# Local attention and two mixing layers on one core: a byte limit on loads in flight, and the constant matmuls that fill gaps

## The chip, the core and the metric

The kernel runs on one core of a Trainium2 chip. The core's engines run side by side and wait for each other only through semaphores: TensorE (PE, with its weight loads shown apart as PEld), VectorE (DVE), ScalarE (ACT), GpSimd (POOL) and SyncE (SP), which here issues every DMA. The metric is the device time of one execution in microseconds (us), as the median of several runs.

## What is computed

The reference chains three layers over 2 sequences of 768 positions and 512 channels (8 heads of 64). Cut to what matters:

```python
k_sum = k.reshape(B, H, nb, 32, D).max(axis=3)       # 24 blocks of 32 keys
v_sum = v.reshape(B, H, nb, 32, D).mean(axis=3)
scores = concat(window of |i-j| < 16, q @ k_sum.T + log(32))
x = softmax(scores) @ concat(v, v_sum)               # heads side by side: 512 channels
theta = x @ w_theta
y = w_tok_r @ (x * cos(theta)) + w_tok_i @ (x * sin(theta))
u = x + y;  x = u + relu(u @ w_ch)
h = gelu(x @ w_in);  u, v = halves(h);  v = normalised(v) * g
out = x + (u * (w_sg @ v + b_sg)) @ w_out
```

The large products are made of three matmuls each (high by high, high by low, low by high parts), lines 352 to 354 of the kernel.

## The kernel before, in words

The work is cut into named steps. Each step has an engine, and one long text, PLAN, lists all steps in the order in which they are issued; `play` goes through it and calls each step's function. Every engine works off its own steps strictly in that order, and an instruction that waits holds up all behind it on its engine. SP's queue is such an engine too: a load that waits holds up all later loads.

Attention handles eight pairs of heads (0 to 7; 0 to 3 are the first sequence), each in two halves of the sequence. For pair p and half h the steps are: loads `kp`, `vTp`, `qp_h`, `vp_h` (384 KB, 384 KB, 192 KB, and two of 97 and 194 KB); `ksp` on DVE, the maxima over blocks of 32 keys (line 514); `Sp_h` on PE, the scores (`scores`: 4 matmuls that write the mask, line 558, then 24 on q and k, line 565, then 24 on q and `ksp`, line 572, as the trace counts them); `m` and `d` on DVE (lines 578 and 599), `e` on ACT (line 607), `PT` on PE (transposes, line 613), `Pt` (their copies out), `O` on PE (line 627), `n` on DVE and `X` on PE (line 649). `vs`, `vp`, `vm`, `vr` carry the block means of v from POOL through PE and ACT into the tiles that `O` reads. From about 41 us the steps `th` (x by w_theta) run between those of attention, and from 70 us those of the token mix (`y`). The loads of weights are `wth`, `wr`, `wi` and `wri`; each is followed by `t` on ACT (line 459) and `r` on DVE (line 466), which put the number together from its two 16-bit parts.

Three things in this stage are touched by the change:

- Loads. Each is a plain `nc.sync.dma_start` (lines 453, 480, 498, 500, 503 and 509). There are eight DMA semaphores, used in turn, so a load waits until the eighth load ahead of it has landed; that is the only limit on loads in flight, apart from buffers that have to come free.
- `fill` (function `filler`, line 405): 8 matmuls of 512 columns on a tile of zeros, right at PE's start. Nothing reads their result. Every `S` step stands behind it on PE.
- `idle0` to `idle4` (function `keep_busy`, line 411): matmuls of 480 columns on constant tiles, whose result nothing reads either. `IDLE` says how many each has: 8, 1, 2, 5, 1. `idle0` stands behind the fifth score step `S1_0`, `idle1` and `idle2` among the first transposes, `idle3` ahead of `S3_0`, `idle4` ahead of `O3_1`.

Of the kernel before, what the change touches and what calls it, by code (L numbers as in the profile page):

```python
# [58 lines left out]
d3_0_0.V.294 m3_0_1.V.2 Pt2_1_0.A.528 vT1.S.696 d3_0_1.V q3_1.S.672 S3_1.P.2.7 e1_0.A PT1_0_0.P.1
vs1.G.6 PT1_0_1.P.3 m3_1_0.V.3 d3_1_0.V.339 vT2.S.624 vp1.P.6 vs2.G.5 vp2.P.4 m3_1_1.V.2 d3_1_1.V  # L60
wth0t.A.0 Pt0_0_1.A.72 e2_0.A PT2_0_0.P.0 vm1.A.1 wth1d.S.896 v0_0.S.847 v0_1.S.798 v1_1.S.1103
v1_0.S.1054 wth3d.S.990 vr0_0.G Pt1_0_0.A.774 vr0_1.G PT2_1_1.P.6 O0_0_0.P.1 v2_0.S.1295 vr1_0.G
O0_0_1.P vp3.P.5 wth1t.A.1 O0_1_0.P.2 O0_1_1.P Pt2_0_0.A.504 n0_0.V.4.198 vr1_1.G O1_1_0.P.0
vm2.A.0 e3_0.A PT3_0_0.P.7 PT3_0_1.P.4 Pt1_0_1.A.0 PT2_0_1.P.1 v2_1.S.1246 vr2_1.G vm3.A.1
# [6 lines left out]
th0_1.P n2_1.V.2 v3_1.S.1655 vr3_1.G idle4.P.5 O3_1_0.P.5 n3_0.V.4 O3_1_1.P X2_1.P.7 xe2_0.A
X3_0.P.1 wth3r.V.1504 th1_1.P th2_1.P xe0_1.A wri2d.S.1591 wi0t.A.1 wth2l.V xh0_1.A.720 q7_0.S.1567
k5.S.1872 n3_1.V.4 xh2_0.A.144 xe1_1.A wr0t.A.0 X3_1.P.5 wri1d.S.1808 k4.S.1760 ks4.V.2 xe3_0.A
wth3h.G.64 S4_0.P.1.0 xl2_0.G xl0_1.G th0_2.P xe2_1.A S4_1.P.7.2 vT4.S.2064 xe3_1.A ks5.V.4
wri0d.S.2000 xh3_0.A.672 wr0r.V.1472 m4_0_0.V.3 wth3l.V d4_0_0.V.1427 wri0t.A.2 xl3_0.G m4_1_0.V.2
m4_0_1.V.3 th1_2.P th2_2.P vs4.V.5 th1_3.P th0_3.P th4_0.P.1 d4_0_1.V vp4.P.0 xh3_1.G.528
# [1008 lines left out]
```

## Time and profile before

| | |
|---|---|
| three runs, median | 386.76 us (386.74 to 387.22) |
| the profiled execution's own time | 386.78 us |
| its span, first to last instruction | 384.9 us |
| PE busy (matmuls) | 371.5 us, 97% |
| DVE, POOL, ACT busy | 281.9, 219.9, 171.4 us |
| DMA | 40.5 MB, mean 105 GB/s |

The span is 1.9 us shorter than the execution's time, which also has a start and an end around it. The page cuts the span into 40 slices of 9.6 us. In the first six slices the DMA engines are nearly always busy (77% to 100%, 258 to 376 GB/s), and from the eighth on they are mostly idle. PE's clock shows below full in the first, second and third slice and is full from there. The last stage of the page, the chain of work that ended last, has PE in 88% of it.

### The profile page before, as it was taken

How to read it: one execution, taken by the hardware profiler on the slowest of the kernel's cores; microseconds unless marked ns; L12 is line 12 of the kernel's file. 1: busy time of each engine (PE TensorE's matmuls, PEld its weight loads, DVE VectorE, ACT ScalarE, POOL GpSimd, SP SyncE). 2: the span in 40 equal slices, each digit the busy share in tenths (PEclk: the TensorE clock that was granted, in tenths of full speed). 3: DMA queues.
4: the chain of work that ended last, by engine and by line, in shares of the span. 5: the costliest groups of instructions: out<-in, count | busy, mean ns of one | idle time of the engine just before them, and what ended most of it. 6: DMA issues, size and time to landing. Idle time of an engine off the chain costs nothing.

```text
span 384.9 us, 7757 instructions
## 1 busy us (share of the span) xinstructions
PE 371.5 (97%) x3073; PEld 333.3 (87%) x3073; DVE 281.9 (73%) x468; ACT 171.4 (45%) x321; POOL 219.9 (57%) x227
## 2 busy tenths in 40 slices
PE   6798999999999999999999999999999999999995
PEld 3577877988888888888889998899899999999994
DVE  4848899898797416954279999979655665368984
ACT  1258778987888635211033436545235102223510
POOL 5656585967454588639545336356632377683440
PEclk9689999999999999999999999999999999999999
DMA  7989997050632230000175350000001000000116
GB/s 269 376 258 346 353 336 232 22 179 6 214 111 72 93 128 35 2 2 2 54 261 190 109 177 3 0 2 1 2 0 41 2 0 2 0 2 0 41 43 246
DMA packets 16483, 40.50 MB, mean 105 GB/s; under 512 B 2240, under 2 KB 7872, under 8 KB 16448
## 3 DMA queue, kind: packets, MB, share of 16 engines
q1 hardware_dynamic: 16448, 40.01, 30.7%
q8 instruction: 24, 0.39, 0.4%
q14 instruction: 11, 0.09, 0.1%
HBM read 36.86 MB, written 3.15 MB: 104 GB/s over the span
## 4 chain that ended last, share of the span: by engine, by line
PE 88%; DVE 6%; issue 2%; ACT 2%; DMA 1%; SPq 0%; DVEq 0%; ACTq 0%
PE bank L352 25%; PE bank L353 25%; PE bank L354 24%; PE bank L627 3%; PE bank L613 3%; PE bank L565 2%; PE bank L649 1%; PE bank L414 1%; PE bank L572 1%; DMA page0F<-in_kT_dram 1%; DVE xT L899 1%; DVE page8R L347 1%; PE bank L558 1%; DVE page7R L347 1%; DVE page12F L813 0%
## 5 line engine op out<-in xcount | busy, mean ns | idle before, releaser
L578 DVE TENSOR_REDUCE small<-bank 128x3 f32<-128x360 f32 x32 | 16.4, 524 | 5.8 <-PE bank L572 5.7
L742 DVE TENSOR_TENSOR xT<-bank,xT 128x512 f32<-128x512 f32 (+1 forms) x16 | 8.3, 547 | 6.5 <-PE bank L354 6.5
L956 ACT ACTIVATE page6F<-bank 128x384 f32<-128x384 f32 x8 | 3.9, 489 | 18.8 <-PE bank L354 18.8
L347 POOL TENSOR_TENSOR page3R<-xT,page3R 128x384 fp32r<-128x384 f32 x6 | 6.8, 1128 | 8.3 <-ACT page3R L339 5.7
L347 POOL TENSOR_TENSOR page2R<-xT,page2R 128x384 fp32r<-128x384 f32 x7 | 7.1, 1025 | 6.5 <-ACT page2R L339 4.2
L973 DVE SCALAR_TENSOR_TENSOR page1F<-bank,g_sb,page10F 128x384 f32<-128x384 f32 x8 | 4.7, 613 | 8.3 <-PE bank L354 8.3
L339 ACT ACTIVATE page10R<-page4F 128x512 fp32r<-128x512 f32 (+1 forms) x2 | 1.5, 740 | 20.0 <-PE bank L353 19.9
L979 POOL TENSOR_TENSOR page1F<-page1F,page6F 128x384 f32<-128x384 f32 x6 | 6.6, 1113 | 5.9 <-DVE page1F L973 4.7
L347 POOL TENSOR_TENSOR page2R<-page9F,page2R 128x512 fp32r<-128x512 f32 x6 | 8.7, 1446 | 1.7 <-ACT page2R L339 1.5
L341 POOL TENSOR_SCALAR page2R<-page9F 128x512 fp32r<-128x512 f32 (+1 forms) x4 | 2.7, 672 | 11.8 <-PE bank L354 9.8
L347 POOL TENSOR_TENSOR page1R<-page9F,page1R 128x512 fp32r<-128x512 f32 x2 | 4.6, 2312 | 7.2 <-ACT page1R L339 7.2
L352 PE MATMUL bank<-page0R,page2R 128*128 128x512 f32 (+1 forms) x21 | 8.5, 405 | 0.0
L347 POOL TENSOR_TENSOR page8R<-page10F,page8R 128x512 fp32r<-128x512 f32 (+1 forms) x3 | 4.6, 1522 | 6.3 <-ACT page8R L339 6.3
L354 PE MATMUL bank<-page0R,page2R 128*128 128x512 f32 (+1 forms) x21 | 7.8, 373 | 0.0
L607 ACT ACTIVATE page1F<-page1F 128x720 f32<-128x720 f32 x4 | 3.2, 800 | 10.4 <-DVE page1F L599 10.4
L353 PE MATMUL bank<-page0R,page2R 128*128 128x512 f32 (+1 forms) x21 | 7.8, 371 | 0.0
L558 PE MATMUL bank<-maskb,identb 64*64 64x288 bf16 x64 | 5.2, 315 | 2.0 <-DVE identb L390 2.0
L466 DVE SCALAR_TENSOR_TENSOR page9F<-page9F,stage 128x512 int32<-128x512 int32 x2 | 1.4, 690 | 7.7 <-POOL page1R L347 7.7
L339 ACT ACTIVATE xT<-bank 128x384 f32<-128x384 f32 x11 | 5.2, 490 | 3.8 <-PE bank L649 3.8
L347 POOL TENSOR_TENSOR page3R<-page4F,page3R 128x512 fp32r<-128x512 f32 x2 | 2.6, 1308 | 7.1 <-ACT page3R L339 7.1
L459 ACT ACTIVATE stage<-page11F 128x512 f16<-128x512 bf16 x8 | 6.2, 786 | 0.9 <-DVE page7F L466 0.9
L1000 POOL TENSOR_TENSOR page10F<-page10F,xT 128x384 f32<-128x384 f32 x3 | 3.6, 1184 | 5.2 <-ACT page10F L339 5.2
(1066 smaller groups left out, 1627.9 us busy)
## 6 DMA issues: line engine op xcount, KB each, us to landing
page11F<-in_w_rT_dram SPq DMA_DIRECT2D x3, 511.8 KB, 5.3
page11F<-in_w_iT_dram SPq DMA_DIRECT2D x3, 511.8 KB, 5.4
page13F<-in_w_in_dram SPq DMA_DIRECT2D x3, 511.8 KB, 5.2
out_dram<-page10F SPq DMA_DIRECT2D x7, 192.0 KB, 2.0
page6F<-in_w_in_dram SPq DMA_DIRECT2D x2, 511.8 KB, 3.4
out_dram<-page1F SPq DMA_DIRECT2D x5, 192.0 KB, 2.1
page6F<-in_vW_dram SPq DMA_DIRECT2D x4, 193.5 KB, 4.3
page0F<-in_kT_dram SPq DMA_DIRECT2D x2, 384.0 KB, 5.0
```

What stands on the lines that cost most here:

```text
L339: ACT.activation(dst, src, AF.Copy)
L347: EN[e].tensor_tensor(out=lo, in0=src, in1=hi.bitcast(F32), op=ALU.subtract)
L352: PE.matmul(ps, ah, bh, start=first, stop=False, skip_group_check=True)
L353: PE.matmul(ps, ah, bl, start=False, stop=False, skip_group_check=True)
L354: PE.matmul(ps, al, bh, start=False, stop=last, skip_group_check=True)
L558: PE.matmul(s3(h)[sl(ab, 64), :, :WK], identb[rr, rr], maskb[rr, m:m + 3], start=True, stop=False, skip_group_check=True)
L565: PE.matmul(s3(h)[sl(ab, 64), t, :WK], q[rr, sl(2 * t + ab, 64)], k[rr, FIRST[w]:FIRST[w] + WK], start=False, stop=True, skip_group_check= ...
L578: op(f"m{u}_{h}", "V", lambda e, h=h: DVE.tensor_reduce(out=T(f"m{u}_{h}"), in_=s3(h), axis=AX.X, op=ALU.max, negate=True), after=[f"S{u}" ...
L613: PE.transpose(T(f"PT{u}_{h}")[:WC, sl(t)], T(f"P{u}")[:, 360 * h + t * WC:360 * h + (t + 1) * WC], ident)
L627: PE.matmul(ps[64 * ab:64 * ab + 64, o:o + 65], sb[:WC, t * P + 64 * ab:t * P + 64 * ab + 64], v[:WC, c:c + 65], start=True, stop=True)
L742: DVE.tensor_tensor(out=dst, in0=ps, in1=dst, op=ALU.add)
L979: op(f"gm{b}_{th}_{f}", "VG", lambda e, gf=gf, s=s, ut=ut: EN[e].tensor_tensor(out=T(gf)[:, s], in0=T(gf)[:, s], in1=T(ut), op=ALU.mult), ...
```

## The change

A new constant, `FLIGHT`, and a function `fetch` that all the loads on lines 453, 480, 498, 500, 503 and 509 now go through (those of g, of `w_sg` and `b_sg`, and the stores, do not). `fetch` issues the load and then counts back over the loads before it, newest first: as soon as those counted make 850,000 bytes, the next older one is made a condition, and this load waits until that one has landed. So when a load is issued, the loads ahead of it that may still be on their way are as many as it takes to reach 850,000 bytes. The wait for the eighth load back stays.

`fill` becomes 80 matmuls of 48 columns, each with its own load of 128 columns of weights, on the same tile of zeros. `IDLE` goes from (8, 1, 2, 5, 1) to (4, 1, 3): `idle0` has 4, the one that stood between `PT0_0_0` and `PT0_1_0` is gone, the next has 1 in place of 2, the one ahead of `S3_0` has 3 in place of 5, and the one ahead of `O3_1` is gone. The order of all other steps is as it was.

```diff
-IDLE = (8, 1, 2, 5, 1,)
+FLIGHT = 850_000
+
+IDLE = (4, 1, 3,)
...
-m2_1_1.V.0 m1_0_1.V.3 d2_1_1.V idle0.P.3 PT0_0_0.P.4 m1_0_0.V.1 idle1.P.3 PT0_1_0.P.1 e1_1.A
-idle2.P.3 PT1_1_0.P.5 Pt0_1_0.A.0 vT3.S.222 d1_0_0.V.2715 d1_0_1.V vT0.S.528 k3.S.480 ks3.V.1
+m2_1_1.V.0 m1_0_1.V.3 d2_1_1.V idle0.P.3 PT0_0_0.P.4 m1_0_0.V.1 PT0_1_0.P.1 e1_1.A idle1.P.3
+PT1_1_0.P.5 Pt0_1_0.A.0 vT3.S.222 d1_0_0.V.2715 d1_0_1.V vT0.S.528 k3.S.480 ks3.V.1 PT0_0_1.P.0
...
+    flying = []
+
+    def fetch(dst, src):
+        i = nc.sync.dma_start(dst, src)
+        i = getattr(i, "ins", i)
+        left = FLIGHT
+        for n, name in reversed(flying):
+            if left <= 0:
+                tc.add_manual_dep(i, name, mybir.DependencyInfo(
+                    mybir.DependencyClass.Sync, mybir.DependencyReason.DATA), reason="flight")
+                break
+            left -= n
+        flying.append(((2 if dst.dtype == I16 else 4) * math.prod(dst.shape), i.name))
...
     def filler(e):
         ps, warm = T("warmb"), T("warm", BF16)
-        for j in range(8):
-            PE.matmul(ps, warm[:, :P], warm[:, P:640], start=True, stop=True)
+        for j in range(80):
+            PE.matmul(ps[:, :48], warm[:, :P], warm[:, P:P + 48], start=True, stop=True)
...
-                nc.sync.dma_start(raw[:, c:c + n - 1], w[:, 1:])
+                fetch(raw[:, c:c + n - 1], w[:, 1:])
...
-        op(f"k{p}", "S", lambda e: nc.sync.dma_start(T(f"k{p}"), kT[b, r]),
+        op(f"k{p}", "S", lambda e: fetch(T(f"k{p}"), kT[b, r]),
```

On SP's queue the loads stand in the same order; what they wait for differs. Before, from the fourth DMA on (in `[waits ...]` the semaphore of the load that must have landed; in_kT is a `k`, in_qT a `q`, in_vT a `vT`, in_w_theta a `wth`):

```order
L498 DMA page0F<-in_kT_dram 128x768
L503 DMA page0F<-in_qT_dram 128x384 x3
L503 DMA page1F<-in_qT_dram 128x384
L500 DMA page1F<-in_vT_dram 128x768 [waits DMAHW0_49]
L500 DMA page2F<-in_vT_dram 128x768 [waits DMAHW1_49]
L498 DMA page2F<-in_kT_dram 128x768 [waits DMAHW2_49]
L503 DMA page1F<-in_qT_dram 128x384 [waits DMAHW3_49]
L453 DMA page2F<-in_w_theta_dram 128x2047 [waits DMAHW4_49]
```

And now (all loads carry the line of `fetch`):

```order
L353 DMA page0F<-in_kT_dram 128x768
L353 DMA page0F<-in_qT_dram 128x384 [waits DMAHW0_49]
L353 DMA page0F<-in_qT_dram 128x384
L353 DMA page0F<-in_qT_dram 128x384 [waits DMAHW1_49]
L353 DMA page1F<-in_qT_dram 128x384 [waits DMAHW2_49]
L353 DMA page1F<-in_vT_dram 128x768
L353 DMA page2F<-in_vT_dram 128x768 [waits DMAHW4_49]
L353 DMA page2F<-in_kT_dram 128x768 [waits DMAHW6_49]
L353 DMA page1F<-in_qT_dram 128x384 [waits DMAHW7_49,DMAHW3_49]
L353 DMA page2F<-in_w_theta_dram 128x2047 [waits DMAHW0_49]
```

The fifth load waits for the first now, where it waited for none, and the load of weights (in_w_theta) waits for the ninth, four loads ahead of it, where it waited for the fifth.

On PE, among the first transposes (L613 before and L631 now are `PT` steps, L414 and L432 the `idle` ones). Before, behind the last matmul of `idle0`:

```order
L414 MATMUL bank3_66<-maskb_91,identb_90 128x480
L613 MATMUL bank4_67<-ident_89,page1F_191 120x128 x3
L414 LDWEIGHTS identb_90
L414 MATMUL bank3_66<-maskb_91,identb_90 128x480
L613 MATMUL bank1_64<-ident_89,page1F_191 120x128 x3
```

And now:

```order
L432 MATMUL bank3_66<-maskb_91,identb_90 128x480
L631 MATMUL bank4_67<-ident_89,page1F_263 120x128 x3
L631 MATMUL bank1_64<-ident_89,page1F_263 120x128 x3
L432 LDWEIGHTS identb_90
L432 MATMUL bank3_66<-maskb_91,identb_90 128x480
```

The second transpose step stands right behind the first. On PE's list of instructions the 72 more matmuls of `fill` and their 72 weight loads come first, so everything behind them stands 144 places later, less two for each `idle` matmul that is gone ahead of it.

## Rows read from the trace of the kernel before

**Rows 1.** The page, parts 1 and 4: busy time, and the chain by engine.

```profile
PE 371.5 (97%) x3073; PEld 333.3 (87%) x3073; DVE 281.9 (73%) x468; ACT 171.4 (45%) x321; POOL 219.9 (57%) x227
PE 88%; DVE 6%; issue 2%; ACT 2%; DMA 1%; SPq 0%; DVEq 0%; ACTq 0%
```

**Rows 2.** By stretch: length, busy (x instructions) by engine, clock, DMA share, GB/s.

```profile
7.00:12.95 5.95, 5.93 (x214) 5.56 (x214) 4.63 (x9) 0.68 (x1) 2.37 (x4) 0.71 1.05 403
15.35:20.50 5.15, 5.15 (x56) 3.19 (x57) 4.25 (x9) 0.80 (x1) 3.41 (x9) 0.50 1.01 320
20.50:30.00 9.50, 9.50 (x200) 7.80 (x198) 4.57 (x10) 6.46 (x15) 4.33 (x8) 0.94 0.84 260
30.00:47.30 17.30, 16.09 (x253) 13.72 (x251) 15.19 (x37) 13.79 (x29) 11.29 (x13) 1.00 1.02 355
100.00:384.90 284.90, 279.39 (x1571) 258.05 (x1565) 200.65 (x305) 104.40 (x195) 152.86 (x130) 1.00 0.17 58
```

**Rows 3.** Timeline, PE to 37 us: start, length, instruction, [idle before, releaser].

```profile
1.71 0.13 PEld L408 LDWEIGHTS <-page14F 128*128 128x128 bf16 x2 [1.71 <-DVE page14F L367]
1.72 3.29 PE L408 MATMUL bank<-page14F 128*128 128x512 bf16 x8 [1.72 <-DVE page14F L367]
2.12 0.15 PEld L408 LDWEIGHTS <-page14F 128*128 128x128 bf16 x1 [0.28 <-issue]
...
6.97 0.32 PE L558 MATMUL bank<-maskb,identb 64*64 64x288 bf16 x4 [1.97 <-DVE identb L390]
...
15.33 1.07 PE L565 MATMUL bank<-page0F 64*64 64x96 f32 x19 [2.41 <-issue]
...
36.66 0.92 PE L627 MATMUL bank<-page6F,page2F 120*64 120x65 f32 x23 [1.21 <-issue]
```

**Rows 4.** The chain that ended last, to 48 us: start, length, what; load `k1`, `idle` matmuls.

```profile
1.24 4.45 DMA page0F<-in_kT_dram
...
17.14 3.31 PE bank L414 x8
...
21.10 0.40 PE bank L414
...
21.95 0.41 PE bank L414 x2
...
25.31 1.01 PE bank L414 x5
...
43.80 0.22 PE bank L414
```

**Rows 5.** By stretch, PE and weight-load counts between the two stops; and DMA queues.

```profile
15.30:36.60 21.30, 20.11 (x376) 15.83 (x376) 15.07 (x36) 13.53 (x29) 13.11 (x23) 0.85 0.93 301
...
q8 instruction: 24, 0.39, 0.4%
```

**Rows 6.** DMA issues: count, KB each, us to landing; the third and fourth near their issue.

```profile
page14F<-in_kT_dram SPq DMA_DIRECT2D x1, 384.0 KB, 2.9
page4F<-in_w_theta_dram SPq DMA_DIRECT2D x1, 511.8 KB, 9.6
...
page9F<-in_kT_dram SPq DMA_DIRECT2D x1, 384.0 KB, 6.6
...
page12F<-in_w_rT_dram SPq DMA_DIRECT2D x1, 511.8 KB, 8.8
```

**Rows 7.** Timeline around `S4_0`: the issue of its load `k4`, `ks4` and `ks5`, `S4_0`.

```profile
36.26 0.43 SPq L498 DMA_DIRECT2D page9F<-in_kT_dram  x1
...
45.81 1.80 DVE L514 TENSOR_REDUCE small<-page9F 128x24 f32<-128x768 f32 x2
...
47.95 0.48 PE L572 MATMUL bank<-small,page8F 64*64 64x24 f32 x24
```

**Rows 8.** Timeline, DVE's waits for PE in the score stage.

```profile
16.62 0.53 DVE L599 TENSOR_TENSOR page0F<-bank,small 128x360 f32<-128x360 f32 x1 [0.87 <-PE bank L565]
...
24.18 0.97 DVE L578 TENSOR_REDUCE small<-bank 128x3 f32<-128x360 f32 x2 [3.40 <-PE bank L572]
...
27.49 0.53 DVE L578 TENSOR_REDUCE small<-bank 128x3 f32<-128x360 f32 x1 [1.46 <-PE bank L572]
```

**Rows 9.** Timeline: the load `wr1`, its steps on ACT and DVE, DVE's next waits.

```profile
47.26 0.74 SPq L453 DMA_DIRECT2D page12F<-in_w_rT_dram  x1
...
58.95 0.79 ACT L459 ACTIVATE stage<-page12F 128x512 f16<-128x512 bf16 x1
...
60.32 0.69 DVE L466 SCALAR_TENSOR_TENSOR page7F<-page12F,stage 128x512 int32<-128x512 int32 x1 [0.18 <-issue]
...
72.32 0.56 DVE L344 COPY xT<-bank 128x384 f32<-128x384 f32 x1 [0.81 <-PE bank L649]
```

More of the change, by code (lines that the diff above doesn't have):

```diff
@@ L59 @@
[L59 to L64, printed above, removed]
@@ L71 @@
[L71 to L76, printed above, removed]
@@ new lines @@
+PT1_1_0.P.5 Pt0_1_0.A.0 vT3.S.222 d1_0_0.V.2715 d1_0_1.V vT0.S.528 k3.S.480 ks3.V.1 PT0_0_1.P.0
+q2_0.S.198 S2_0.P.1.3 Pt0_0_0.A.123 m2_0_0.V.3 sets.G PT0_1_1.P.6 Pt1_1_0.A.456 PT1_1_1.P.5 vs3.G.4
+m2_0_1.V.2 d2_0_0.V.27 vs0.G.5 vp0.P.4 d2_0_1.V e2_1.A Pt0_1_1.A.96 Pt1_1_1.A.552 vm0.A.0
+wth0d.S.392 q3_0.S.744 PT2_1_0.P.2 idle2.P.6 S3_0.P.4.5 m3_0_0.V.3 d3_0_0.V.294 m3_0_1.V.2
+Pt2_1_0.A.528 vT1.S.696 d3_0_1.V q3_1.S.672 S3_1.P.2.7 e1_0.A PT1_0_0.P.1 vs1.G.6 PT1_0_1.P.3
+m3_1_0.V.3 d3_1_0.V.339 vT2.S.624 vp1.P.6 vs2.G.5 vp2.P.4 m3_1_1.V.2 d3_1_1.V wth0t.A.0
@@ new lines @@
+Pt0_0_1.A.72 e2_0.A PT2_0_0.P.0 vm1.A.1 wth1d.S.896 v0_0.S.847 v0_1.S.798 v1_1.S.1103 v1_0.S.1054
+wth3d.S.990 vr0_0.G Pt1_0_0.A.774 vr0_1.G PT2_1_1.P.6 O0_0_0.P.1 v2_0.S.1295 vr1_0.G O0_0_1.P
+vp3.P.5 wth1t.A.1 O0_1_0.P.2 O0_1_1.P Pt2_0_0.A.504 n0_0.V.4.198 vr1_1.G O1_1_0.P.0 vm2.A.0 e3_0.A
+PT3_0_0.P.7 PT3_0_1.P.4 Pt1_0_1.A.0 PT2_0_1.P.1 v2_1.S.1246 vr2_1.G vm3.A.1 v3_0.S.1197 X0_0.P.5
+wth0r.V.88 wth1r.V.1165 vr2_0.A Pt2_0_1.A.456 vr3_0.G O1_0_0.P.3 O1_0_1.P xe0_0.A e3_1.A O1_1_1.P
+n0_1.V.4.800 n1_0.V.2 n1_1.V.4 O2_1_0.P.5 O2_0_0.P.1 O2_0_1.P wth1h.G.2688 PT3_1_0.P.2 Pt2_1_1.A.0
@@ new lines @@
+O2_1_1.P Pt3_0_0.A.48 O3_0_0.P.7 n2_0.V.2 Pt3_0_1.A.24 O3_0_1.P wth2d.S.1472 wr0d.S.1408
+wth0h.G.576 X1_1.P.0 X1_0.P.4 X2_0.P.1 xh0_0.G.720 xl0_0.G wi0d.S.1344 wth2t.A.1 wth0l.V
+wth2r.V.1071 wth1l.V PT3_1_1.P.3 q4_1.S.966 wth3t.A.0 Pt3_1_0.A.1128 xe1_0.A xh1_0.A.672 xl1_0.G
+X0_1.P.2 Pt3_1_1.A.1104 th1_0.P.4 th0_0.P.6 wth2h.A.0 th2_0.P.3 q4_0.S.1704 th0_1.P n2_1.V.2
+v3_1.S.1655 vr3_1.G O3_1_0.P.5 n3_0.V.4 O3_1_1.P X2_1.P.7 xe2_0.A X3_0.P.1 wth3r.V.1504 th1_1.P
+th2_1.P xe0_1.A wri2d.S.1591 wi0t.A.1 wth2l.V xh0_1.A.720 q7_0.S.1567 k5.S.1872 n3_1.V.4
@@ new lines @@
+xh2_0.A.144 xe1_1.A wr0t.A.0 X3_1.P.5 wri1d.S.1808 k4.S.1760 ks4.V.2 xe3_0.A wth3h.G.64 S4_0.P.1.0
+xl2_0.G xl0_1.G th0_2.P xe2_1.A S4_1.P.7.2 vT4.S.2064 xe3_1.A ks5.V.4 wri0d.S.2000 xh3_0.A.672
+wr0r.V.1472 m4_0_0.V.3 wth3l.V d4_0_0.V.1427 wri0t.A.2 xl3_0.G m4_1_0.V.2 m4_0_1.V.3 th1_2.P
+th2_2.P vs4.V.5 th1_3.P th0_3.P th4_0.P.1 d4_0_1.V vp4.P.0 xh3_1.G.528 m4_1_1.V.6 d4_1_0.V.1763
+xh1_1.A.480 d4_1_1.V xl3_1.G wri1t.A.0 th2_3.P q6_1.S.1543 q6_0.S.1736 v4_0.S.1951 xl1_1.G
+q5_0.S.1927 S5_0.P.7.5 th4_1.P xh2_1.A.432 th5_0.P.2 xl2_1.G wr0h.A.960 wi0r.V.2080 e4_0.A
@@ new lines @@
+wri0r.V.1504 m5_0_1.V.6 m5_0_0.V.2 wr0l.G kk0.A.1696 d5_0_0.V.2019 th4_2.P PT4_0_0.P.7 vm4.A.1
+th4_3.P th5_1.P wri1r.V.1472 kk1.A.1664 wr2d.S.2240 e4_1.A d5_0_1.V PT4_0_1.P.5 th5_2.P wi1d.S.2176
+wi1t.A.2 PT4_1_0.P.0 vr4_0.G th5_3.P wr2t.A.1 wr3d.S.2112 kk2.A.1395 vT5.S.2448 Pt4_0_0.A.1371
+th3_0.P.7 rr1.V.352 vT6.S.2400 wr1d.S.2336 PT4_1_1.P.4 v4_1.S.2639 th3_1.P th3_2.P wr1t.A.0
+wi1r.V.1840 wr1r.V.1440 rr2.V.320 vr4_1.A rr0.V.1664 wri0h.G.1024 vs5.V.6 vp5.P.6 wr1h.G.1088
+Pt4_0_1.V.2312 v5_0.S.2590 wi2d.S.2526 k6.S.912 vs6.V.2 ks6.V.6 Pt4_1_0.A.1347 wi1h.G.128
@@ L479, in load @@
             for s in srcs:
-                nc.sync.dma_start(raw[:, c:c + s.shape[1]], s)
+                fetch(raw[:, c:c + s.shape[1]], s)
                 c += s.shape[1]
@@ L497, in at_pair @@
         b, r = divmod(p, NP)
-        op(f"k{p}", "S", lambda e: nc.sync.dma_start(T(f"k{p}"), kT[b, r]),
+        op(f"k{p}", "S", lambda e: fetch(T(f"k{p}"), kT[b, r]),
            new=[(f"k{p}", "F", 4 * S)], size=(P * S * 4, 1))
-        op(f"vT{p}", "S", lambda e: nc.sync.dma_start(T(f"vT{p}"), vT[b, r]),
+        op(f"vT{p}", "S", lambda e: fetch(T(f"vT{p}"), vT[b, r]),
            new=[(f"vT{p}", "F", 4 * S)], size=(P * S * 4, 1))
         for hf in range(2):
-            op(f"q{p}_{hf}", "S", lambda e, hf=hf: nc.sync.dma_start(
+            op(f"q{p}_{hf}", "S", lambda e, hf=hf: fetch(
                 T(f"q{p}_{hf}"), qT[b, r, :, 384 * hf:384 * hf + 384]),
@@ L508, in load_v @@
                 for rr in (slice(0, 32), slice(32, WK)):
-                    nc.sync.dma_start(T(f"v{p}_{hf}")[rr], vW[b, r, rr, VH * hf:VH * hf + VH])
+                    fetch(T(f"v{p}_{hf}")[rr], vW[b, r, rr, VH * hf:VH * hf + VH])
             op(f"v{p}_{hf}", "S", load_v, new=[(f"v{p}_{hf}", "F", 4 * VH)],
```

25 lines of the change are left out of this document (4 added, 21 removed).

## The prediction

> **What bounds the kernel now.** I read the page first. PE is busy for 371.5 of 384.9 us and has 88% of the chain [rows 1]; from 100 us to the end it is busy for 279.4 of 284.9 us at full clock, with little DMA [rows 2]. So a microsecond that PE gains early is kept to the end, if the other engines and the loads can follow, and one that it loses early is lost. The change touches the first 45 us, so I read those by stretch: from 7 to 20.5 us the granted clock is 0.71 and 0.50, after that 0.94 and 1.00; the loads run at 260 to 403 GB/s all the time [rows 2]. Then the timeline for PE's pauses [rows 3]: 1.97 us behind `fill`, until `identb` is there; 2.41 us in the middle of a score step, until 15.33 us; 1.21 us in the middle of an `O` step, until 36.66 us. The last two are put down to "issue", that is to nothing the profile shows. Then the chain, for what the `idle` matmuls cost [rows 4].
>
> What the two "issue" pauses are: queue q8 brings "instruction" data, 24 packets of 0.39 MB in all [rows 5]. PE has 2 x 3073 = 6146 matmuls and weight loads [rows 1]; 0.39 MB over 6146 is 63 bytes each, so a packet is some 256 of them. Between the pauses PE does 376 + 376 = 752 [rows 5], close to three packets. I take the pauses for PE's program running out while the next packet stands behind loads in the DMA engines.
>
> **The `idle` matmuls.** Four of `idle0`'s eight go (3.31 / 8 x 4 = 1.66 us), then 0.40, one of two (0.41 / 2 = 0.20), two of five (1.01 / 5 x 2 = 0.40) and the last (0.22) [rows 4]: 2.9 us, all on PE's path. What they hide is the low clock: PE ran at half rate from 15.35 to 20.50 us with them [rows 2], and may stay there longer without. 5.95 us at a mean of 0.71 hold 2 x 0.29 x 5.95 = 3.5 us at the low level; one more such stretch costs half of it, 1.7 us.
>
> **`fill`.** Now it takes 3.29 us for 4096 columns, 1.25 columns per ns, which is the lower level, 1.2 GHz, and ends at 5.0 us; PE then stands idle until 6.97 [rows 3]. The new one has 80 x 48 = 3840 columns, 3.1 us if only columns count: then it ends at 4.8 and nothing changes. But each matmul has its own weight load. Two together took 0.13 us, 0.065 each, and one alone 0.15 [rows 3]; 80 of them are 5.2 or 12.0 us, ending at 6.9 or 13.7. I take 6.9, from the row in which loads follow each other: free, since `identb` ends the wait at 6.97, and PE has no pause ahead of the scores. The other end of the range, a gain, is that the scores from 7 us then run at full clock: at 0.71 they took 5.93 us, so up to 1.7 us.
>
> **The pauses for instructions.** The fetch stands among the loads: a load took 2.9 us from issue to landing when it was first and up to 9.6 later [rows 6]. With 850 KB ahead of it, at 355 GB/s (30 to 47 us, [rows 2]), it is 2.4 us until these are through. So I expect the 1.21 us to go, and the 2.41 us to move: 72 more matmul pairs put the end of the packet into the third score step, and a shorter queue leaves about half, a gain of 1.2. Bounds: nothing and all 3.6 us.
>
> The Trainium skill speaks against this part: DMA: Bandwidth & Descriptors, section on queues, rings and completion order, says that each DMA engine takes turns between the queue rows that it has work for, so that instructions on their own row should not stand behind the loads on another. No row here shows the turns; by it the pauses would stay. That case is the third rival.
>
> **What PE would gain by 44 us.** 2.9 + 1.2 + 1.2 = 5.3 us, or 4.1 with the pause of 1.21 alone. DVE can follow: it waited for PE 0.87 + 3.40 + 1.46 = 5.7 us up to 27.5 us [rows 8].
>
> **Where the loads stop it.** `S4_0` needs `k4` and the maxima `ks4`. `k4` was issued at 36.26 and took 6.6 us, landing at 42.9 [rows 6, 7]; two maxima take 1.80 us, so `ks4` is there 0.9 later and the part of `S4_0` that reads it can start at 43.9 at the earliest. It started at 47.95 [rows 7]. PE can therefore be at most 4.05 us ahead here, if `k4` lands when it did. This is below 5.3, so the loads decide.
>
> **What the limit does to the loads.** They land one behind the other, so fewer in flight need not make them later, as long as the queue never empties. A load alone takes 2.9 us for 384 KB, of which 1.1 us is its transfer at 355 GB/s, so 1.8 us are delay. 850 KB last 2.4 us at that rate: enough, with 0.6 us to spare. But SP now issues later, one by one, after landings, and the many small `v` loads may not be ready when the large ones are through. I take one issue, 0.43 us [rows 7], as the lag; the bounds are 0.5 us earlier and the 7.9 us of the second rival. So PE is 4.05 - 0.43 = 3.6 us ahead at `S4_0`, and stands waiting there for about 5.3 - 3.6 = 1.7 us.
>
> **Behind `S4_0`.** The next tight load is `wr1`: issued at 47.26, landed 8.8 us later at 56.1, read by ACT at 58.95 [rows 6, 9]: 2.9 us of slack, 2.5 with the lag. DVE's step behind it follows; it has 0.18 of its own wait, and 0.81 of waiting for PE at 72.32 [rows 9], so PE feels it from 2.5 + 0.18 + 0.81 = 3.5 us on. Later loads wait for buffers that come free earlier with the compute. The other changes (72 matmuls more in the count, `fetch` itself) cost nothing: the one is in `fill`, the other is done when the program is built.
>
> **Sum.** 3.5 us off the profiled execution's 386.78, which stands 0.02 above the median: 383.3 us. With the lag of the loads between -0.5 and +1.2 us, 382.4 to 384.2.
>
> **Rivals.**
> *The clock falls again*, because PE stands idle for some 1.7 us ahead of `S4_0`, or without the `idle` matmuls for longer than the margin covers. For it: the pauses of 1.97 and 2.41 us stand beside the only low stretches [rows 2, 3]. Against: the pause of 1.21 us left the clock at 1.00. Price 1.7 us: 385.0.
> *The limit starves the loads, and the kernel is slower.* If 850 KB move only once per 2.9 us, the time of the first load, the rate is 293 in place of 355 GB/s; the 37.2 us from 5.7 (the landing of the second load, 1.24 + 4.45, [rows 4]) to 42.9 become 45.1, and `k4` lands 7.9 us late. Less the 4.05 of slack this is 3.8 us: 390.6. It decides from 4.05 us late, a rate of 320 GB/s. Against it: the new load adds to the 850 KB, and loads overlap. The Trainium skill has a rule for it: DMA: Bandwidth & Descriptors, section on the anatomy of one DMA, gives 2.0 us plus bytes over 436 GB/s, with half the bandwidth at some 860 KB. As an estimate by that page, were its fixed time paid for every 850 KB, the loads would run at 215 GB/s and the kernel would take about 407 us. The first load's delay, 1.8 us, agrees with the page's 2.0, but the rows have loads landing one on the other, 355 GB/s from 30 to 47 us [rows 2].
> *The pauses stay.* Then PE gains only the 2.9 us of the `idle` matmuls: 383.9.
> *`fill` is too long.* At 0.15 us a piece it ends at 13.7, 6.7 us after `identb`: 2.9 + 1.2 + 2.4 (that pause would fall into the delay) - 6.7 leaves -0.2, 387.0, the same within what is measured.
> *The loads land earlier*, because the start, where the second load took longest, gains too: up to 1.3 us more, 382.0.
>
> **How the numbers follow.** Forecast 0.52, clock 0.12, starved loads 0.09, pauses stay 0.13, long `fill` 0.06, earlier loads 0.08. A difference of 0.2%, 0.8 us, is about what a measurement of this kernel can tell from none. Faster: 0.52 + 0.12 + 0.13 + 0.08 = 0.85; same 0.06; slower 0.09. The range leaves out the slow and the same case, 0.15, and goes from 382.0 to 385.6 (the clock case with 0.6 of lag).
>
> **What would show it.** Right: PE busy without a pause from 2 to 8 us, no "issue" pause near 36 us, the first transposes 4 to 5 us earlier, a wait of PE ahead of `S4_0` for `k4` or `ks4`, loads at some 350 GB/s until 60 us with landings 3 to 4 us after issue, and everything from 100 us on shifted by the same amount. Wrong: loads at 300 GB/s or less between 10 and 45 us; `S0_1` well after 7 us; a low clock after 25 us; or PE reaching `S4_0` less than 3.5 us earlier, so that the loads do not decide.

## The result, and the profile after

The changed kernel takes 392.73 us (median of 4 runs, 390.32 to 396.48), the kernel before on the same chip 386.94 us (386.74 to 387.22). The ratio is 1.013, with a 95% interval of 1.008 to 1.018: slower by some 5 us, where 383.3 us was forecast. (The ratio, here and below, is taken from means and not from the two medians, and it leaves out the execution of 396.48 us, a slow one in which PE's clock was lower.) The profiled execution took 392.27 us with a span of 390.4 us, 5.5 us more than that of before.

The page of the kernel after, parts 1 and 4, against [rows 1]: busy time by engine, and the chain of work that ended last by engine.

```profile
PE 371.3 (95%) x3136; PEld 336.0 (86%) x3136; DVE 279.5 (72%) x468; ACT 171.5 (44%) x321; POOL 220.4 (56%) x227
PE 73%; DMA 15%; DVE 7%; issue 2%; SPq 1%; ACT 0%; DVEq 0%; ACTq 0%
```

PE has as much work as before (371.3 us). What is new is DMA in the chain: 15% of the span where it was 1%. Where that sits, the chain itself shows. Its part from 28 to 70 us (start, length, what):

```profile
28.12 4.33 DMA page6F<-in_vW_dram
32.47 4.55 DMA page7F<-in_w_rT_dram
37.03 3.62 DMA page8F<-in_vW_dram
40.67 4.37 DMA page9F<-in_kT_dram
45.06 4.22 DMA page10F<-in_vT_dram
49.30 5.49 DMA page10F<-in_vW_dram
54.80 4.46 DMA page11F<-in_w_iT_dram
59.28 0.33 SPq L353
59.66 6.41 DMA page12F<-in_w_rT_dram
66.15 0.79 ACT stage L477
66.96 0.69 DVE page7F L484
67.66 0.60 DVE page1F L695
68.25 0.60 DVE page8F L695
68.85 0.87 DVE small L539
69.77 0.28 PE bank L546
```

Nearly each load starts within 0.1 us of the landing of the one ahead in the chain, because its issue waited for that landing. From 1.70 us on thirteen loads stand in the chain like this, 59.3 us in all. In the trace of before one load (`k1`) was in the chain up to 100 us, [rows 4].

By stretch, against [rows 2] (start and end, length, busy us and instructions of PE, PEld, DVE, ACT and POOL, clock, DMA share, GB/s; the two stretches from 44.7 us are PE's wait at `S4_0` and what came behind it):

```profile
7.00:12.95 5.95, 5.41 (x185) 5.30 (x182) 4.19 (x8) 0.44 (x1) 2.23 (x4) 1.00 0.98 323
...
20.50:30.00 9.50, 8.30 (x206) 7.23 (x207) 8.47 (x19) 7.07 (x16) 7.66 (x12) 1.00 0.73 228
30.00:47.30 17.30, 11.98 (x173) 10.00 (x169) 9.43 (x25) 10.62 (x23) 9.52 (x12) 1.00 0.87 281
...
44.70:48.10 3.40, 0.01 (x4) 0.00 (x0) 0.08 (x1) 0.71 (x2) 2.45 (x3) 1.00 0.92 279
48.60:55.40 6.80, 6.77 (x98) 5.24 (x89) 5.19 (x10) 2.82 (x5) 3.26 (x3) 0.50 0.87 264
...
100.00:390.40 290.40, 284.85 (x1610) 262.37 (x1604) 203.54 (x314) 107.95 (x203) 156.88 (x132) 1.00 0.18 61
```

The loads run at 323 in place of 403 GB/s from 7 us, at 228 in place of 260, at 281 in place of 355 from 30 to 47 us. The DMA engines have more gaps: their share is 0.73 and 0.87 where it was 0.84 and 1.02. PE's busy time from 30 to 47.3 us falls from 16.09 to 11.98 us. From 100 us on PE is idle for 5.5 us, as it was before.

The clock in the first row is not to be trusted: no record of it lies ahead of 11 us in this execution, and the column then reads 1.00. The instructions tell: the 24 matmuls of the first two score steps (the shape of line 583, 64x96) last 1.18 us, where they take 0.67 us later, so PE ran at the lower level until 11 us.

The timeline of PE to 49 us, against [rows 3] (start, length, instruction, and in brackets the idle time before it and what released it):

```profile
1.72 3.38 PE L426 MATMUL bank<-page14F 128*128 128x48 bf16 x80 [1.72 <-DVE page14F L385]
6.53 0.46 PE L576 MATMUL bank<-maskb,identb 64*64 64x288 bf16 x4 [1.43 <-DVE identb L408]
...
12.08 0.36 PE L590 MATMUL bank<-small,page0F 64*64 64x24 f32 x12 [0.54 <-issue]
...
16.44 0.27 PE L631 MATMUL bank<-ident,page1F 128*120 128x128 f32 x1 [0.59 <-issue]
22.17 0.31 PE L576 MATMUL bank<-maskb,identb 64*64 64x288 bf16 x2 [0.52 <-issue]
...
32.87 1.27 PE L645 MATMUL bank<-page6F,page2F 120*64 120x65 f32 x36 [2.06 <-POOL page3R L365]
...
48.13 0.87 PE L583 MATMUL bank<-page9F,page8F 64*64 64x96 f32 x24 [3.42 <-DMA page9F<-in_kT_dram]
```

Up to 30 us PE is ahead as forecast: `PT0_0_0` starts at 15.14 us where it started at 20.25, `O0_0_0` at 25.04 where it started at 30.06. Then it stands still 2.06 us until 32.87, and 3.42 us at `S4_0` for `k4`. The profile puts the first of these down to POOL. But what this step needs of POOL by the program, the block means in `page6F`, was written by 29.20 us, while the two loads of `v` that it reads landed at 32.45 and 32.73 us. So it is rather a wait for late loads too, and on the later chip the profile names this load at the same step (1.73 us until 31.16, DMA `page6F<-in_vW_dram`). It costs nothing by itself, since PE then waits for `k4` anyhow. The issues of `k4` and `wr1` against [rows 6] (KB each, us from issue to landing; the first row has two loads):

```profile
page9F<-in_kT_dram SPq DMA_DIRECT2D x2, 384.0 KB, 4.4
...
page12F<-in_w_rT_dram SPq DMA_DIRECT2D x1, 511.8 KB, 6.4
```

Each load is faster than before (4.4 us for 6.6, 6.4 for 8.8), and each lands later, because it is issued later: `k4` is issued at 43.58 and lands at 47.99 us (before 36.26 and 42.82), `wr1` at 59.66 and 66.07 (47.26 and 56.01). What waits for `wr1`, on ACT and then on DVE, against [rows 9]:

```profile
66.15 0.78 ACT L477 ACTIVATE stage<-page12F 128x512 f16<-128x512 bf16 x1 [3.19 <-DMA page12F<-in_w_rT_dram]
66.96 0.69 DVE L484 SCALAR_TENSOR_TENSOR page7F<-page12F,stage 128x512 int32<-128x512 int32 x1 [3.28 <-ACT stage L477]
...
69.77 0.28 PE L546 MATMUL bank<-ident,small 128*24 128x128 f32 x1 [1.47 <-DVE small L539]
```

So the loss adds up at three places. `S4_0` ends at 49.88 us, 1.45 later than before. `S5_0` starts at 58.71 against 54.74, 4.0 later: between the two PE was busy, but its clock was at the lower level, 1.2 GHz, from 48.6 to 55.4 us. And the token mix starts at 76.21 against 70.64, 5.6 later, with the wait for `wr1`. From there to the end nothing more changes (5.5 us at the end).

### The profile page after: what moved, and what is told of

It is laid out like the page before. It is cut to its first block, busy times and chain, and to the rows that moved or that the text cites. A ratio compares the mean times of both kernels' runs of the same rounds, so it can differ in the third digit from the quotient of the medians.

```text
span 390.4 us, 7890 instructions
## 1 busy us (share of the span) xinstructions
PE 371.3 (95%) x3136; PEld 336.0 (86%) x3136; DVE 279.5 (72%) x468; ACT 171.5 (44%) x321; POOL 220.4 (56%) x227
## 4 chain that ended last, share of the span: by engine, by line
PE 73%; DMA 15%; DVE 7%; issue 2%; SPq 1%; ACT 0%; DVEq 0%; ACTq 0%
PE bank L370 23%; PE bank L371 23%; PE bank L372 23%; DMA page1F<-in_qT_dram 2%; PE bank L645 2%; DMA page12F<-in_w_rT_dram 2%; DMA page10F<-in_vW_dram 1%; SPq L353 1%; DMA page3F<-in_qT_dram 1%; DMA page7F<-in_w_rT_dram 1%; DMA page5F<-in_vW_dram 1%; DMA page11F<-in_w_iT_dram 1%; DMA page9F<-in_kT_dram 1%; DMA page6F<-in_vW_dram 1%; DMA page10F<-in_vT_dram 1%
## 5 line engine op out<-in xcount | busy, mean ns | idle before, releaser
L576 PE MATMUL bank<-maskb,identb 64*64 64x288 bf16 x64 | 6.0, 332 | 1.9 <-DVE identb L408 1.4
L370 PE MATMUL bank<-page0R,page3R 128*128 128x384 f32 (+2 forms) x18 | 6.2, 346 | 0.0
L365 POOL TENSOR_TENSOR page3R<-page10F,page3R 128x512 fp32r<-128x512 f32 x2 | 2.9, 1442 | 5.9 <-PE bank L372 5.9
```

Of the source, the lines that this page charges most:

```text
L370: PE.matmul(ps, ah, bh, start=first, stop=False, skip_group_check=True)
L576: PE.matmul(s3(h)[sl(ab, 64), :, :WK], identb[rr, rr], maskb[rr, m:m + 3], start=True, stop=False, skip_group_check=True)
```

## The experiments

The theories. **A**: the limit slows the loads, and what waits for them (`S4_0`, `wr1`) is the loss. Its sharper form (A1, where a text tells it from others) is that the bytes on their way, over the time that a load takes from issue to landing, set the rate. **B**: the loss comes from PE's part, the new `fill` or the shorter idle table. Later texts name their own rivals.

Every ratio below is to the kernel before in the same rounds on the same chip. Three chips were used, and the kernel before took 384.2 to 384.9 us there (medians), not 386.9; the record doesn't say which chip the first result came from, and below it is called the first chip.

**No limit.** The changed kernel with a limit that never acts.

```diff
-FLIGHT = 850_000
+FLIGHT = 1_000_000_000
```

> The changed kernel with the limit on loads set so high that it never waits; the new fill and the fewer idle matmuls stay. Theory A (the limit slows the loads, and the loads hold PE up at S4_0 and at wr1): the loads run at some 350 GB/s from 30 to 47 us again, k4 lands at 42 to 43.5 us, PE waits at S4_0 for under 2 us, and the time is 383 to 384.5 us. Rival B (the loss comes from the new fill or from the missing idle matmuls, by the low clock or by other pauses): 389 us or more, with k4 landing where it did before.

384.40 us, ratio 1.001 (0.999 to 1.003). The stretch from 30 us, and the timeline of PE at `S4_0`, in this kernel:

```profile
30.00:47.30 17.30, 15.65 (x294) 13.47 (x291) 15.76 (x34) 13.33 (x28) 10.48 (x12) 1.00 1.00 348
```

```profile
44.42 0.32 PE L576 MATMUL bank<-maskb,identb 64*64 64x288 bf16 x4
44.57 0.67 PE L583 MATMUL bank<-page9F,page8F 64*64 64x96 f32 x24
45.06 0.48 PE L590 MATMUL bank<-small,page8F 64*64 64x24 f32 x24
```

348 GB/s again, `k4` lands at 42.91 us, and no idle time stands in front of `S4_0`. The loss is gone, and with it B as its cause: the new `fill` and the shorter table are both still in. But the forecast gain isn't there either.

**The limit alone.** The kernel before with `fetch`, old `fill` and old table.

```diff
-for j in range(80):
-    PE.matmul(ps[:, :48], warm[:, :P], warm[:, P:P + 48], start=True, stop=True)
+for j in range(8):
+    PE.matmul(ps, warm[:, :P], warm[:, P:640], start=True, stop=True)
...
-IDLE = (4, 1, 3,)
+IDLE = (8, 1, 2, 5, 1,)
...
```

> The kernel before with the limit of 850 KB alone: old fill, old idle matmuls. Theory A: the loads run at some 285 GB/s, k4 lands at 47 to 48.5 us and wr1 near 66 us as in the changed kernel; since they decide, the time is as in the changed kernel, 390 to 394 us. Rival B: within 1 us of before, 386 to 388 us.

391.88 us, ratio 1.020 (1.014 to 1.026): the whole loss, from the limit alone. The profile is of the longest execution of the four (394.64 us). In it the loads run at 260 GB/s, `k4` lands at 51.97 us and `wr1` at 67.65, all worse than expected. PE's wait in this kernel, in the timeline:

```profile
52.10 1.24 PE L583 MATMUL bank<-page9F,page8F 64*64 64x96 f32 x24 [4.37 <-DMA page9F<-in_kT_dram]
```

**Other sizes of the limit.** The changed kernel with 1.7, 1.2 and 0.5 MB.

```diff
-FLIGHT = 850_000
+FLIGHT = 1_700_000
```

> The changed kernel with 1700 KB in place of 850 KB. Theory A in its form A1 (a load takes some 4 us from issue to landing among others, so bytes in flight over 4 us set the rate; 1700 KB would allow over 400 GB/s): full rate of some 350 GB/s, 383 to 384.5 us. Form A2 (each wait of SP for a landing costs, whatever the size): rate still under 320 GB/s and over 387 us. Rival B: as in the changed kernel, 390 to 394 us.

> The changed kernel with 1200 KB in place of 850 KB. A1: what is in flight is some 1200 to 1600 KB, over 4 to 4.4 us 320 to 360 GB/s, k4 lands 1 to 3 us later than before, 384 to 387 us. A2: no better than the changed kernel, over 389 us. Rival B: 390 to 394 us.

> The changed kernel with 500 KB in place of 850. Theory A (bytes on their way over the time that a load takes set the rate): 200 to 260 GB/s between 30 and 47 us, k4 at 50 to 58 us, 394 to 408 us, ratio 1.025 to 1.06. Rival (the cost of the limit is the wait at each issue, so much per load and whatever the limit's size): the same as with 850 KB, 275 to 290 GB/s, ratio 1.015 to 1.025.

The table puts them beside the others. Rate: 30 to 47.3 us. Time of a load: the mean from issue to landing of all loads issued from 12 to 45 us of that profile. The last column but one is the product of the two. The profiles come from several chips, one execution each.

| limit | ratio (95%) | `k4` lands, us | GB/s | time of a load, us | on the way, MB | 2.1 us + 1.85 us per MB |
|---|---|---|---|---|---|---|
| none | 1.001 (0.999 to 1.003) | 42.9 | 348 | 5.95 | 2.07 | 5.9 |
| 1.7 MB | 1.000 (0.997 to 1.003) | 43.4 | 326 | 5.59 | 1.82 | 5.5 |
| 1.2 MB | 1.004 (1.001 to 1.008) | 45.0 | 319 | 5.01 | 1.60 | 5.1 |
| 0.85 MB (first chip) | 1.013 (1.008 to 1.018) | 48.0 | 281 | 4.24 | 1.19 | 4.3 |
| 0.5 MB | 1.056 (1.051 to 1.061) | 56.3 | 223 | 3.71 | 0.83 | 3.6 |

The rows from which the rates for 1.7, 1.2 and 0.5 MB are:

```profile
30.00:47.30 17.30, 16.89 (x298) 14.21 (x297) 14.53 (x35) 13.02 (x28) 11.67 (x13) 1.00 0.97 326
...
30.00:47.30 17.30, 14.28 (x232) 11.86 (x232) 11.83 (x30) 11.09 (x24) 9.90 (x12) 0.99 0.94 319
...
30.00:47.30 17.30, 13.35 (x182) 11.53 (x178) 11.91 (x27) 9.78 (x21) 8.29 (x10) 0.85 0.71 223
```

With less on the way a load does get faster, but not in proportion: from 2.07 to 0.83 MB, a factor of 2.5, its time falls by a factor of 1.6, and the rate by the rest. A straight line through the five, the last column, has 2.1 us that don't go with what is on the way. Its two numbers are rough: rate and time in the table are of different stretches. With both from 12 to 45 us the line is 2.0 us plus 2.0 us per MB, with both from 30 to 47.3 us 1.8 plus 2.1, and with the bytes on their way added up load by load over that last stretch 1.3 plus 2.3. The kernel with the limit alone lies 0.4 us above the line in the table (4.77 us at 1.24 MB).

This is A1, though with a time that isn't fixed at 4 us: 1.7 MB gave 326 GB/s and not the expected 350, at 5.59 us a load. It speaks against A2 (each wait of SP costs, whatever the size), by which 1.7 and 1.2 MB would have lost as much, and against the rival of the last text: a cost per issue whatever the size would have left 0.5 MB at some 281 GB/s. The loss of 0.4% with 1.2 MB is no larger than what the kernel before showed against itself (below), but there PE's wait for `k4` is seen in the trace, 2.62 us until 45.09. What is on the way is some 0.3 to 0.4 MB more than the limit says, up to 1.2 MB, since the new load comes on top. Theory A's own figure for 0.5 MB, 394 to 408 us, holds 405.57.

The Trainium skill has a rule for one DMA that GpSimd issues (DMA: Bandwidth & Descriptors, section on the anatomy of one DMA): some 2.0 us fixed, plus bytes over 436 GB/s, half the bandwidth at about 860 KB. Here SP issues, and the bytes are those of all loads on the way. The numbers are alike all the same: 1.3 to 2.1 us fixed, and 1.85 to 2.3 us per MB against the 2.3 that 436 GB/s make.

**The kernel before and the changed one, again, on a chip of the later ones.** No edits.

> The kernel before, unchanged, looked at on the chip on which the next three run, because the runs without a limit stood level with it on one chip though they lay 2.6 us under it on another. Theory A (the loads are what S4_0 waits for, and 850 KB in flight move them too slowly): ratio 1.00; k4 lands at 42.5 to 43.5 us here too, and S4_0 starts 0 to 2 us later than the 44.42 us of the run without the limit, by how long TensorE's clock was low in the first 25 us of this execution. If S4_0 starts at 44 to 45 us here, the whole gain of small pairs and fewer idle matmuls ends at the wait for k4; if at 46 to 47.5 us, the early gain is real in the profile and must show in the times of the next runs. Theory B (the early part of TensorE decides everywhere): S4_0 starts at 47.3 us as in the first trace, 2.9 us behind the run without the limit, and the time is 2.6 us more than that run's.

> The changed kernel, unchanged, on the same chip as its neighbours. Theory A: ratio 1.010 to 1.025 to the kernel before, k4 at 47 to 49 us, wr1d at 65 to 68 us, 270 to 300 GB/s between 30 and 47 us, as on the first chip. Rival (the first chip was a bad draw for the changed kernel): ratio 1.000 to 1.005 and k4 below 45 us.

Before against itself: 384.36 us, ratio 0.996 (0.992 to 1.000), which shows what ratio can come out of nothing. The changed kernel: 392.75 us, ratio 1.020 (1.015 to 1.025), with PE's wait of 4.06 us for `k4` at `S4_0`, 291 GB/s from 30 to 47.3 us, and `wr1` at 63.09 us, earlier than expected. So the first chip was no bad draw for the changed kernel. What differed there was the kernel before. In its trace on this chip the eight matmuls of `idle0`, and the third part of `S4_0`, stand like this on PE:

```profile
15.37 1.79 PE L414 MATMUL bank<-maskb,identb 128*128 128x480 bf16 x8
...
44.13 0.48 PE L572 MATMUL bank<-small,page8F 64*64 64x24 f32 x24
```

The eight take 1.79 us, where they took 3.31 in the execution that the prediction read [rows 4]: there the clock was at half from 15.35 to 20.50 us [rows 2], here it isn't. `S3_1` starts at 23.6 us in place of 27.2, the last part of `S4_0` at 44.13 in place of 47.95 [rows 7], and the span is 381.1 us in place of 384.9. `k4` lands at 41.61 us, so the slack that was 4.05 us there is some 1.5 us here by the same reckoning. Both theories of the text on this kernel had `k4` or `S4_0` (here 43.49 us) later.

**The parts of PE alone.** The shorter idle table without limit and with the old `fill`; and the 80 small matmuls without limit and with the old table.

```diff
-FLIGHT = 850_000
+FLIGHT = 1_000_000_000
...
-for j in range(80):
-    PE.matmul(ps[:, :48], warm[:, :P], warm[:, P:P + 48], start=True, stop=True)
+for j in range(8):
+    PE.matmul(ps, warm[:, :P], warm[:, P:640], start=True, stop=True)
```

> The changed kernel without the limit and with the old eight large matmuls in the fill, so that only the shorter idle table and the order that belongs to it stay. Theory A: k4 lands at 42.5 to 43.5 us, S4_0 starts within 1 us of 44.4 us, the ratio to the run with the small pairs and no limit is within 0.3% of 1.000, so the ratio to the kernel before is 0.997 to 1.004. The rival that the small pairs in the fill are worth something of their own (a shorter fill, program pages passed earlier): 1 to 3 us over the run without the limit, ratio 1.003 to 1.008.

382.66 us, ratio 0.995 (0.992 to 0.998): by its interval a gain of 0.5%, some 1.8 us. But the kernel before against itself came out at 0.996 in the same rounds, so this run alone doesn't show that the table gains anything. The expectation missed: it had this kernel within 0.3% of the one with the small pairs, and that is 0.6% off (on another chip). `k4` landed at 41.68 us and `S4_0` began at 40.51, not near 44.4; its second part, on PE, had to wait for `k4`:

```profile
41.81 0.73 PE L583 MATMUL bank<-page9F,page8F 64*64 64x96 f32 x24 [0.99 <-DMA page9F<-in_kT_dram]
```

```diff
-FLIGHT = 850_000
+FLIGHT = 1_000_000_000
...
-IDLE = (4, 1, 3,)
+IDLE = (8, 1, 2, 5, 1,)
...
```

> The kernel before with the 80 small matmuls in the fill and nothing else: the old idle table, no limit. So far the shorter idle table alone gave a ratio of 0.995 and both together 1.001. Theory F (the small pairs cost: 72 more pairs bring TensorE's program pages forward, and in the trace of both together TensorE waited at matmul 349 as well as 222, where with the old fill it had the next pause only at 598): a pause of 0.5 to 2.7 us at matmul 349 here too, and a ratio of 1.002 to 1.008. Rival G (the fill is worth nothing either way; the two ratios differ by the spread of these runs): ratio 0.997 to 1.002. Rival H (my prediction's step, each page passed earlier is a gain): ratio 0.993 to 0.997.

385.22 us, ratio 1.003 (1.000 to 1.006). The timeline of PE:

```profile
12.62 0.53 PE L590 MATMUL bank<-small,page0F 64*64 64x24 f32 x12 [0.77 <-issue]
19.01 0.38 PE L631 MATMUL bank<-ident,page1F 128*120 128x128 f32 x2 [0.57 <-issue]
```

The second pause is the one at matmul 349 (counted from the program's start) that theory F expected. The gain (H) is excluded by the interval. Between a small cost (F) and none (G) the interval doesn't decide clearly, and one profile can't tell the pause from the clock, which was low to 16 us in this execution (the 22 matmuls of line 583 at 14.88 us took 1.26 us, and 0.70 us in the kernel with both parts and no limit). Small pairs bring nothing that shows, and may cost up to 2 us; why stays open.

**The limit on the loads behind `k4` alone.**

```diff
-        left = FLIGHT
+        left = FLIGHT if len(flying) > 46 else 1_000_000_000
```

> The changed kernel with the limit on the loads behind k4 alone: the first 47 loads are issued as without it. Theory A: k4 lands at 42 to 43.5 us and S4_0 starts at 43 to 45.5 us as without a limit; behind it the loads run at 280 to 300 GB/s and wr1d lands at 58 to 61 us in place of 56.4, with a wait of 0 to 3 us for it: ratio 1.001 to 1.010, which puts half or more of the whole loss (1.020) on the loads up to k4. Rival (the loss comes about behind k4, and S4_0's wait is given back later): ratio 1.015 to 1.025.

387.58 us, ratio 1.010 (1.005 to 1.015). `k4` lands at 42.09 us and `S4_0` starts at 43.03, as without a limit. Behind it the loads run at 285 GB/s, and ACT waits for `wr1`, then PE:

```profile
47.30:60.00 12.70, 12.57 (x109) 9.88 (x107) 8.88 (x15) 6.57 (x13) 5.16 (x6) 1.00 0.87 285
```

```profile
59.11 0.79 ACT L477 ACTIVATE stage<-page12F 128x512 f16<-128x512 bf16 x1 [4.05 <-DMA page12F<-in_w_rT_dram]
...
62.73 0.39 PE L546 MATMUL bank<-ident,small 128*24 128x128 f32 x1 [2.36 <-DVE small L539]
```

So the limit costs some 1% by way of `wr1` even when `S4_0` is on time, and PE's clock adds to it: it is at the lower level from 62.65 us, where this wait ends, to 66.07. That the other half of the 2% comes about at `S4_0` follows by subtraction, between runs on different chips, and the intervals are wide. `wr1` landed at 59.0 us, 2.6 later than without a limit. There is hardly slack for it, though [rows 9] had shown 2.9 us: without a limit ACT already waited 0.32 us for it.

**Loads in the order of need.** No limit, the new table; `wri1` is issued behind `k4`, and `vT6`, `q6`, `wr3`, `wri2`, `q7` behind `v4_1` and `q5_1`. First with the new `fill`, then with the old.

```diff
-th2_1.P xe0_1.A wri2d.S.1591 wi0t.A.1 wth2l.V xh0_1.A.720 q7_0.S.1567 k5.S.1872 n3_1.V.4
-xh2_0.A.144 xe1_1.A wr0t.A.0 X3_1.P.5 wri1d.S.1808 k4.S.1760 ks4.V.2 xe3_0.A
+th2_1.P xe0_1.A wi0t.A.1 wth2l.V xh0_1.A.720 k5.S.1872 n3_1.V.4
+xh2_0.A.144 xe1_1.A wr0t.A.0 X3_1.P.5 k4.S.1760 wri1d.S.1808 ks4.V.2 xe3_0.A
...
```

> The changed kernel without the limit, and with loads issued in another order on SP: wri1d (64 KB rows for a later stage) behind k4, and vT6, q6, wr3d, wri2d and q7, which are needed later, behind v4_1 and q5_1; the bytes are the same. Theory A in its sharper form (without the limit the wait for k4 is what S4_0 ends on, and it is the order of the loads that sets k4): k4 lands at 39.5 to 41.5 us in place of 42.9, S4_0 starts at 42 to 43.5 us in place of 44.4, wr1d lands 1 to 4 us earlier than 56.4, and the time is 1 to 3 us under the kernel before on this chip: ratio 0.992 to 0.997. Rival C (S4_0 is held by VectorE or TensorE as well, k4 only came last by a little): k4 lands earlier but S4_0 moves by under 0.5 us, ratio 0.999 to 1.003. Rival D (a load moved behind is itself needed: wri2d, q6 or vT6): a new wait at their users, ratio above 1.003.

> The shorter idle table with the old fill and no limit, and with the loads in the order in which they are needed (wri1d behind k4; vT6, q6, wr3d, wri2d and q7 behind v4_1 and q5_1). Theory A: with the table alone VectorE still waited 2.6 us for k4 ahead of S4_0; with k4 landing at 40 us or earlier in place of 41.7 this wait falls by 1 to 2 us and the ratio is 0.988 to 0.994. Rival: VectorE or TensorE comes to S4_0 no earlier than k4 does in most executions, and the ratio stays at 0.994 to 0.998, as with the table alone.

With the new `fill`: 383.77 us, ratio 0.997 (0.995 to 1.000), inconclusive; its profile is of the longest execution of the ten (386.21 us), with PE's clock low near 15 and near 40 us, and though `k4` landed at 40.4 us DVE came to it only at 45.7, and `S4_0` started at 47.19. With the old `fill`: 381.69 us, ratio 0.994 (0.992 to 0.997), below both kernels, but level with the shorter table alone (0.995). `k4` lands at 37.96 us, `S4_0` starts at 42.86 and waits for nothing, `wr1` lands 7 us earlier than in the table's own run (48.66 against 55.99). The ratio lies on the border of what theory and rival expected; by the profile it is the rival: once `k4` comes in time, PE's own work is next. That the order of the loads gives anything is not shown.

## Why the prediction was wrong

**The step that failed** is "what the limit does to the loads". It took a lag of 0.43 us; `k4` landed 5.2 us later and `wr1` 10.1. The reasoning set the 2.4 us that 850 KB last at 355 GB/s against the 1.8 us of delay of a load alone, and concluded that the queue never empties. But a load among others takes longer from issue to landing than one alone: 4.24 us under the limit. At 355 GB/s over 4.24 us 1.5 MB would have to be on the way; the limit lets 1.2 MB, which last 3.4 us at that rate. The DMA engines did stand still in between (share 0.87 from 30 us on, where it was 1.02). The rows for this product were read and not multiplied: 355 GB/s [rows 2] by the 6.6 us of `k4` [rows 6] are 2.3 MB on the way before, and the change admits half of it. Part of the 4.24 us lies inside each load: the trace has sixteen updates of its semaphore for every load, and from 12 to 45 us the first comes 2.71 us after the issue, the last 4.24 (means of 34 loads). The limit waits for the last, 1.5 us behind the first. What draws them apart, and how the rest is shared between other loads' packets and a delay of its own, the runs don't show; the straight line only suggests it.

**The rival of starved loads** had the mechanism: 293 GB/s were forecast by it and 281 measured, 390.6 us and 392.27. It had a chance of 0.09. It was held back by two sentences "against it", that the new load comes on top and that loads overlap. Both are true, and both are in the 1.2 MB. That its rate came so near is in part luck: it took 0.85 MB in 2.9 us, and measured were 1.19 MB in 4.24 us, both 1.4 to 1.5 times as much. Its price came out by parts that it didn't have: `k4` was 5.2 us late and not 7.9, since `k1` landed earlier (4.9 us, before 5.7) and the loads from there to `k4` took a sixth longer (43.1 us for 37.1), not a fifth; the rest came from the clock and from `wr1`. Its point of decision, 320 GB/s, doesn't contradict the sizes: 319 GB/s cost 0.4%, 326 nothing, and no run is fine enough to tell more.

**The range** of the sum let the lag go up to 1.2 us, and no row stands behind that figure; the bound that the text itself had named was 7.9 us. Three of its four signs of being wrong came: loads at 300 GB/s or less, a low clock after 25 us, and PE at `S4_0` only 2.9 us earlier (44.40 for 47.31).

**The clock** was the first rival, at 1.7 us, and it came true at the place that was named: PE stood idle for 3.42 us until 48.13, and from 48.6 to 55.4 us its clock was at 0.50. 2.5 us of the loss lie there. That the wait brings the low clock is not shown: PE also waited 2.06 us in this execution, and 2.75 us in the kernel without a limit (until 19.43), and the clock stayed at 1.00. It should not have been a rival beside the forecast but part of whatever makes PE wait at `S4_0`.

**The slack** of 4.05 us at `S4_0` was right for that execution, but much of it was made by the low clock of that execution from 15 to 20 us: without it the kernel before has some 1.5 us. This fits that the limit costs 2% on the later chips and 1.3% on the first, and that the forecast gain is not there even with the loads on time: no limit gives 1.001, not the forecast 0.991.

**`idle` matmuls**: -2.9 us forecast, 1.8 us measured with the loads free, of which the spread between runs of one program leaves little. With the loads in the other order it was 0.994 on another chip, so the sign is likely right; the size isn't shown.

**`fill`**: it ended at 5.10 us, near the lower bound (4.8), not at 6.9: 0.042 us a pair. The choice between the bounds was wrong and cost nothing, since `identb` ended the wait in either case (6.53 us). The other bound, that the scores then run at full clock, didn't come true in this trace: they took 1.18 us a step. In others with the new `fill` the clock was full there (from 5.50 to 12.32 us with 1.7 MB), and with the old one it was full from 4.57 to 7.98 us in the first trace, so `fill` doesn't decide it.

**The "issue" pauses**: the one near 36 us went as forecast, but in the kernel without a limit it is gone too, so the limit isn't shown as the reason. The one of 2.41 us became three, 0.54, 0.59 and 0.52 us, each 127 matmuls behind the other, which is 254 instructions and fits packets of some 256. A gain of 0.8 in place of 1.2. The Trainium skill's rule that a DMA engine takes turns between its queue rows (DMA: Bandwidth & Descriptors, section on queues, rings and completion order) had spoken for pauses that stay; no row here shows the turns. The same program without the limit paused 1.56 us at the first of the three places and 2.75 at the second, but the other one without it only 0.77 and 0.57. Over all traces with the new `fill` the first two together come to 0.6 to 1.2 us with a limit of 1.2 MB or less (four traces), and to 1.3 to 4.3 us where none of that size acts so early (five). So the limit does seem to shorten them, as forecast, by one execution each; shortening them by 1 to 3 us is in any case not worth 5.

**What PE would gain by 44 us**: 5.1 us at `PT0_0_0` and 5.0 at `O0_0_0`, by 25 us, where 5.3 were forecast. Right against the first trace, though much of it was the clock there, and none of it could be kept.

**`wr1`** was named as the next tight load, with 2.5 us of slack left. It was late by 10.1 us, so the wait came about as described, through ACT and DVE to PE.

## What to carry to other kernels

Before limiting what is on the way, multiply the rate of the loads by their time from issue to landing: what comes out is what is on the way now, and a limit well below it costs rate. Here it was 2.1 to 2.3 MB; 1.8 MB on the way cost no time that could be measured, and 1.2 MB cost 1.3 to 2%. A shorter queue made each load faster here and all of them later. And take a slack only after looking at whether the clock, or something else that differs from one execution to the next, has made it: here one trace showed 4 us, another 1.5.
